# One channel chunk of an S4 inverse transform: products in fp32, fields summed on VectorE, a quarter of the matmuls

## The chip, the cores and the metric

The kernel runs on one core of a Trainium2 chip. The metric is the device time of one launch in microseconds (us). The core has five engines that run side by side, each in its own program order: TensorE (PE, matmuls; PEld is its weight load), VectorE (DVE), ScalarE (ACT), GpSimd (POOL) and SyncE (SP, which here issues nearly all DMAs). They wait for each other by semaphores.

## The reference

An S4 layer (a long convolution along the sequence, its kernel K built from complex exponentials) with a skip, then an MLP with layer norms, both added to the input. L = 2048, D = 512, N = 128 states, F = 1376.

```python
logdA = dt * A;  dB = dt * Bc
P = jnp.exp(logdA[:, :, None] * l[None, None, :])
K = jnp.einsum("dn,dnl,dn->dl", Cc, P, dB).real
...
Yf = Uf * Kf[None, :, :, :]
y = irfft2(Yf, ...)[:, :, 0, :L]
y = y.transpose(0, 2, 1) + u * Dskip[None, None, :]
...
x = A_u
h = x + _A_ref(_layernorm(x), ...)
h2 = h + _B_ref(_layernorm(h), B_w1, B_b1, B_w2, B_b2)
```

`_B_ref` normalizes once more, multiplies by w1 (512 to 1376), adds b1, takes a gelu, multiplies by w2 (1376 to 512) and adds b2.

## The kernel before

The sequence is cut into two blocks of 1024 rows (b = 0 and 1), the 512 channels into four chunks of 128 (`NCH = 4`, `CW = 128`). The convolution is done in a transformed domain by matmuls with small tables instead of an FFT. Up to about 105 us the kernel builds the convolution's kernel K (sines, exponentials, products: VectorE and ScalarE) and the forward transforms. Then, for each block and chunk, `inverse` multiplies transformed kernel and transformed input and transforms the product back. Block 0 needs one pair of fields (kernel, input). Block 1 needs two pairs, since its rows see both blocks of the input: (KF of block 0, input block 1) and (KF of block 1, input block 0).

`inverse(b, c, pairs, zt, pr)` works in two halves (`fh`) of 8 x 128 columns. A half is, for each pair and for `sw` 0 and 1, one multiply on VectorE of two bf16 fields of 128x1024 (L1193; with `sw` = 1 real and imaginary rows are swapped on one side) into a bf16 product tile. There are four product tiles `PR[0..3]`, used in turn, so a half of block 1 uses all four, and the next half's multiplies wait until TensorE has read them. Then come the matmuls that transform back (L1203): 16 per product tile, 64x128 each, 64 per half in block 1, all summed in one PSUM tile. The signs of the complex product are in the tables: rows r = 0 and 1 of a `sw` = 0 product go with the tables 0 and 1, both rows of a `sw` = 1 product with table 2. ScalarE (L517) or VectorE (L519) moves the PSUM tile to the tile Z, rearranged (128x128x8). After the second half, `turn` (L1219) lets SP issue a transposing DMA from Z to `ZT1[c]`.

When the four chunks of a block are done, `tail` (two per block, `sb`) makes the output of the convolution with the skip from the four ZT tiles (L1278), adds it to the input on VectorE (L1281), takes statistics (L1282, with a small power on POOL, L579), scales (L1293 or L1295) and transposes the result: by TensorE in the first tail of block 0 (L1305), by a `turn` elsewhere. `mlp` then has 11 column pieces of four matmuls each (L1321) with a gelu on ScalarE (L1323), and four row pieces of eleven matmuls each (L1337) with an addition on VectorE (L1339) and the DMAs to the output (L530). The MLP of block 0 is used as TensorE work between and behind the halves of block 1's inverse.

Every operation is recorded first, with a number in the order of recording. Then they are issued in an order written out as a table of numbers, `ORDER`: entry k stands for operation k // 2 on the first or second engine that it may take (k % 2), which settles whether a PSUM evacuation runs on ScalarE or on VectorE. An entry below zero is one "fill": a 128x512 matmul on the identity (L1434) that computes nothing. `SLOTS` gives the PSUM bank of each new PSUM tile. The cost numbers in `add` and its helpers serve the planner that wrote the table; no instruction depends on them.

The calls around the change, block 1's inverse and what follows it:

```python
    for c in range(NCH):
        inverse(1, c, [(KFb[0][c], XBc[c]), (KFb[1][c], XR[c])], ZT1[c], 17 + 0.1 * c)
    load_x(1, 16)
    mlp(0, 1, y2T[1], 18)
    tail(1, 0, y2T[2], 19)
```

Of the kernel before, what the change touches and what calls it, by code (L numbers as in the profile page):

```python
# [20 lines left out]
CW = 128  # L21
# [161 lines left out]
class VS(V):  # L183
# [28 lines left out]
    679, 578, 810, 808, 812, 542, 598, 1073, 510, 322, 624, 1079, -7, -7, -7, 702, 768, 520, 576, 512, 604, 528, 544, 536, 752, 554, 694, 308, 630,
    560, 814, 818, 826, 820, 390, 698, 754, 824, 696, 324, 706, 708, 710, 832, 688, 704, 690, 1082, 1084, 1086, 830, 326, 1080, 712, 868, 572, 700,
    1088, 1091, 822, 872, 750, 398, 564, 714, 716, 718, 720, 722, 874, 870, 834, 724, 1092, 1094, 1096, 888, 884, 1098, 1108, 726, 890, 904, 886, 756,
    880, 732, 1112, 736, 900, 828, 836, 876, 728, 882, 1111, 906, 920, 902, 878, 922, 744, 892, 848, 742, 839, 896, 850, 262, 738, 898, 392, 758,
    1100, 1102, 734, 1105, 730, 740, 932, 916, 788, 934, 918, 776, 912, 914, 1200, 936, 762, 786, 316, 894, 940, 780, 764, 924, 908, 910, 938, 1204,
    942, 944, 926, 856, 840, 1203, 858, 948, 950, 842, 972, 928, 956, 952, 782, 958, 860, 778, 930, 960, 964, 954, 946, 784, 864, 962, 974, 980, 966,
    770, 968, 970, 976, 774, 866, 863, 852, 1210, 982, 1212, 988, 854, 978, 844, 984, 760, 986, 990, 1214, 846, 996, 998, 1012, 772, 1114, 1140, 1142,
    1014, 1106, 1216, 1004, 1218, 1024, 1020, 1220, 1026, 1006, 1016, 1022, 1160, 1000, 992, 1116, 1002, 1124, 1126, 994, 1144, 1163, 1222, 1120,
    1164, 1146, 1122, 1008, 1152, 1225, 1010, 1018, 1028, 1030, 1038, 1032, 1034, 1166, 1156, 1158, 1154, 1206, 1256, 1258, 1260, 1036, 1040, 1048,  # L220
    1044, 1148, 1118, 1150, 1136, 1046, 1050, 1138, 1060, 1262, 1264, 1132, 1134, 1266, 1268, 1208, 1052, 1654, 1226, 1228, 1390, 1042, 1054, 1658,
    1312, 1062, 1271, 1272, 1656, 1231, 1274, 1232, 1392, 1276, 1236, 1394, 1279, 1234, 1652, 1239, 1240, 1242, 1056, 1282, 1284, 1128, 1176, 1178,
    1192, 1194, 1287, 1288, 1172, 318, 1131, 1320, 1322, 1175, 1314, 1188, 1190, 1280, 1168, 1170, 1660, 1662, 1324, 1665, 1327, 1244, 1246, 1316,
    1330, 1318, 1332, 1416, 1302, 1306, 1292, 1338, 1304, 1248, 1252, 1254, 1334, 1290, 1336, 1410, 1340, 1251, 1328, 1342, 1344, 1356, 1298, 1294,
    1296, 1348, 1180, 1196, 1358, 1360, 1182, 1350, 1301, 1376, 1374, 1198, 1362, 1352, 1628, 1366, 1396, 1354, 1368, 1648, 1378, 1650, 1370, 1644,
    1346, 1380, 1631, 1696, 1620, 1647, 1640, 1643, 1372, 1386, 1382, 1364, 1622, 1632, 1635, 1388, 1624, 1384, 1184, 1698, 1418, 1626, 1692, 1694,
    1420, 1666, 1430, 1186, 1426, 1402, 1428, 1422, 1432, 1668, 1670, 1310, 1798, 1308, 1796, 1678, 1636, 1424, 1434, 1436, 1438, 1404, 1440, 1638,
    1700, 1702, 1444, 1706, 1710, 1442, 1446, 1498, 1400, 1457, 1465, 1708, 1704, 1500, 1448, 1674, -2, -2, -2, -2, -2, -2, -2, -2, -2, -2, 1460,
    1712, 1467, 1468, 1802, 1473, 1476, 1676, 1458, 1462, 1452, 1480, 1474, 1398, 1724, 1479, 1718, 1720, 1672, 1470, 1454, 1486, 1722, 1714, 1492,
    1552, 1544, 1482, 1450, 1494, 1726, 1800, 1412, 1730, 1716, 1414, 1554, 1406, 1564, 1566, 1540, 1542, 1734, 1729, 1736, 1568, 1570, 1546, 1536,  # L230
    1538, 1556, 1732, 1680, 1684, 1738, 1683, 1488, 1686, 1558, 1548, 1532, 1688, 1560, 1744, 1746, 1484, 1408, 1550, 1748, 1750, 1740, 1496, 1528,
    1530, 1490, 1502, 1514, 1534, 1752, 1584, 1504, 1506, 1508, 1510, 1586, 1608, 1758, 1690, 1760, 1756, 1562, 1742, 1512, 1516, 1523, 1521, 1754,
    1518, 1762, 1588, 1524, 1764, 1770, 1776, 1772, 1596, 1774, 1610, 1766, 1598, 1600, 1778, 1782, 1572, 1526, 1780, 1590, 1808, 1784, 1844, 1768,
    1804, 1788, 1786, 1790, 1806, 1816, 1792, 1612, 1574, 1576, 1820, 1578, 1810, 1812, 1602, 1824, 1826, 1840, 1794, 1614, 1814, 1908, 1944, 1910,
    1912, 1896, 1822, 1914, 1902, 1962, 1818, 1898, 1904, 1916, 1950, 1842, 1900, 1956, 1592, 1906, 1918, 1920, 1922, 1836, 1952, 1838, 1832, 1828,
    1830, 1580, 1924, 1926, 1958, 1846, 1930, 1928, 1848, 1834, 1932, 1860, 1936, 1872, 1874, 1934, 1938, 1946, 1960, 1941, 1942, 1876, 1850, 1852,
# [1249 lines left out]
```

## Time and profile before

| | us |
|---|---|
| three runs | 243.19, 244.04, 246.56 |
| median | 244.04 |
| profiled execution | 245.59 |
| its span | 243.2 |
| TensorE busy | 215.4 (3696 matmuls) |
| VectorE busy | 179.6 (407 instructions) |
| ScalarE busy | 170.5 (232 instructions) |

The span is what the trace covers; the profiled execution's own time is 2.4 us longer. The page cuts the span into 40 slices of 6.08 us, and a digit is the busy share of an engine in a slice in tenths:

```profile
PE   7559786878988876979998999999999999999994
DVE  6999999999999995659998988797506991213022
ACT  3999999999999956975997987785134402903700
PEclk9999999999999999999999999999999999999999
```

The first 17 slices are the kernel's making and the forward transforms, with VectorE and ScalarE full. Block 0's inverse, tail and first MLP pieces and block 1's forward transforms follow, then from about 159 us (slice 27) on chunks 2 and 3 of block 1's inverse with MLP work, and from 186 us on block 1's tails and the rest of the MLP. "PEclk" is the granted TensorE clock in tenths of full speed.

### The profile page before, as it was taken

The numbers are of one execution on the slowest core, as the hardware profiler recorded it, in microseconds if no ns is written. First come the engines' busy times: TensorE is split into PE (matmuls) and PEld (weight loads), VectorE is DVE, ScalarE is ACT, GpSimd is POOL, SyncE is SP. The second block draws the span as 40 slices with busy tenths as digits, with TensorE's granted clock in tenths as the row PEclk, the third lists the DMA queues.
The fourth block names the chain that finished last, engine by engine and source line by source line (L and its number), as shares of the span: only waits on it lengthen the run. The fifth ranks groups of instructions, "written<-read, shape, count | busy, mean of one in ns | idle before, by whom it ended". The sixth has DMA issues, their size and how long they took to land.

```text
span 243.2 us, 8615 instructions
## 1 busy us (share of the span) xinstructions
PE 215.4 (89%) x3696; PEld 126.2 (52%) x3705; DVE 179.6 (74%) x407; ACT 170.5 (70%) x232; POOL 18.3 (8%) x145
## 2 busy tenths in 40 slices
PE   7559786878988876979998999999999999999994
PEld 2436243656634454755775476655554444444443
DVE  6999999999999995659998988797506991213022
ACT  3999999999999956975997987785134402903700
POOL 8800000011000000300000010010000101000000
PEclk9999999999999999999999999999999999999999
DMA  5121124000013943417899485644514051142303
GB/s 149 34 62 44 38 19 82 20 3 7 3 25 82 214 132 125 125 30 163 231 159 210 121 254 95 214 80 85 99 28 83 0 106 27 41 88 65 86 19 71
DMA packets 42448, 21.40 MB, mean 88 GB/s; under 512 B 30761, under 2 KB 40618, under 8 KB 42410
## 3 DMA queue, kind: packets, MB, share of 16 engines
q1 hardware_dynamic: 42250, 20.79, 38.0%
q8 instruction: 29, 0.48, 0.8%
q10 hardware_dynamic: 160, 0.07, 0.1%
q14 instruction: 9, 0.07, 0.1%
HBM read 10.33 MB, written 4.49 MB: 61 GB/s over the span
## 4 chain that ended last, share of the span: by engine, by line
PE 59%; DVE 26%; DMA 5%; issue 4%; SPq 3%; ACT 1%; DVEq 0%; ACTq 0%
PE ps L1321 16%; PE ps L1337 16%; PE ps L1203 7%; DVE ar L579 5%; DVE ar L519 4%; DMA ar<-ar 4%; PE ps L919 4%; PE ps L940 3%; DVE ar L1010 3%; SPq L530 3%; DVE ar L584 3%; PE ps L1054 3%; DVE ar L1031 3%; PE ps L1278 3%; PE ps L1055 2%
## 5 line engine op out<-in xcount | busy, mean ns | idle before, releaser
L517 ACT CAST ar<-ps 128x1024 bf16<-128x1024 f32 (+4 forms) x66 | 59.0, 941 | 16.7 <-PE ps L1203 7.5
L1323 ACT ACTIVATE ar<-ps,ar 128x512 bf16<-128x512 f32 (+1 forms) x44 | 27.6, 686 | 35.3 <-PE ps L1321 35.3
L1321 PE MATMUL ps<-ar 128*128 128x512 bf16 (+1 forms) x176 | 39.8, 379 | 0.0
L1337 PE MATMUL ps<-ar 128*128 128x512 bf16 (+2 forms) x179 | 38.5, 366 | 0.6 <-issue 0.3
L1339 DVE TENSOR_TENSOR ar<-ps,ar 128x512 bf16<-128x512 f32 (+1 forms) x17 | 10.8, 657 | 36.1 <-PE ps L1337 32.7
L519 DVE CAST ar<-ps 128x1024 bf16<-128x1024 f32 (+5 forms) x29 | 29.2, 1015 | 8.9 <-ACT ar L1029 2.8
L1193 DVE TENSOR_TENSOR ar<-ar 128x1024 bf16<-128x1024 bf16 x48 | 30.7, 685 | 6.5 <-PE ps L1203 6.0
L1337 PEld LDWEIGHTS <-ar 128*128 128x128 bf16 (+1 forms) x187 | 18.0, 98 | 19.6
L1321 PEld LDWEIGHTS <-ar 128*128 128x128 bf16 (+1 forms) x176 | 17.2, 100 | 20.4 <-issue 1.0
L1054 PE MATMUL ps<-ar 128*20 128x33 bf16 x512 | 20.0, 249 | 6.1 <-issue 5.6
L1203 PE MATMUL ps<-ar 64*128 64x128 bf16 x768 | 23.7, 216 | 0.1
L1203 PEld LDWEIGHTS <-ar 64*128 64x128 bf16 x768 | 21.5, 94 | 4.3 <-issue 2.1
L1029 ACT ACTIVATE ar<-ps 128x1024 bf16<-128x1024 int16 x20 | 19.6, 1039 | 3.0 <-issue 2.4
L579 POOL TENSOR_TENSOR ar<-ar 128x4 f32<-128x4 f32 (+1 forms) x6 | 7.4, 1226 | 187.5 <-DVE ar L584 149.3
L1010 DVE TENSOR_TENSOR ar<-ar 128x1024 bf16<-128x1024 bf16 x32 | 21.2, 684 | 0.2
L1055 PEld LDWEIGHTS <-ar 128*20 128x20 bf16 x512 | 17.7, 125 | 6.5 <-issue 6.4
L1055 PE MATMUL ps<-ar 128*20 128x33 bf16 x512 | 20.1, 248 | 0.0
L1054 PEld LDWEIGHTS <-ar 128*20 128x20 bf16 x512 | 17.6, 124 | 3.0 <-DVE ar L1031 1.5
L723 ACT ACTIVATE ar<-ar 128x512 bf16<-128x512 f32 x32 | 18.2, 628 | 0.5 <-DVE ar L565 0.5
L919 PE MATMUL ps<-ar 128*32 128x512 bf16 x256 | 15.7, 380 | 1.4 <-ACT ar L517 0.6
L1027 PE MATMUL ps<-ar 128*32 128x256 f16 (+2 forms) x288 | 13.5, 280 | 2.8 <-ACT ar L1029 2.7
L1031 DVE TENSOR_TENSOR ar<-ar 128x512 bf16<-128x512 bf16 x40 | 15.4, 413 | 0.3
(99 smaller groups left out, 284.6 us busy)
## 6 DMA issues: line engine op xcount, KB each, us to landing
ar<-in_A_u_dram SPq DMA_DIRECT2D x16, 128.0 KB
ar<-in_A_u_dram SPq DMA_DIRECT2D x8, 256.0 KB
out_dram<-ar SPq DMA_DIRECT2D x30, 64.0 KB
ar<-in_B_w_dram SPq DMA_DIRECT2D x4, 344.0 KB
ar<-in_B_w_dram SPq DMA_DIRECT2D x2, 640.0 KB
AK_d<-ar SPq DMA_DIRECT2D x2, 512.0 KB
ar<-AK_d SPq DMA_DIRECT2D x2, 512.0 KB
AKc_d<-ar SPq DMA_DIRECT2D x4, 256.0 KB
```

The lines of the kernel that those rows point to most:

```text
L517: act.copy(out_fn(), in_fn())
L519: dve.tensor_copy(out_fn(), in_fn())
L919: pe.matmul(pst(p)[32 * j:32 * j + 32, 512 * z:512 * z + 512], lhsT=BX.ap()[:, f0 + z, 16 - 16 * c:48 - 16 * c], rhs=src[2 * j + c].ap(), ...
L1010: add("DVE", c_dve(1024, 2), lambda e, lo=lo, rv=rv, sz=sc[z], e0=e0, o0=o0, q=q: dve.tensor_tensor(ent(o0, q, lo, 4, rv), ent(e0, q, lo, ...
L1031: add("DVE", c_dve(512, 2), lambda e, sc=sc, b0=b0, tb=tb, z=z: dve.tensor_tensor(tb[b0:b0 + 4].ap(), EA[c][b0:b0 + 4].ap(), sc[z].ap(), A ...
L1054: pe.matmul(o, lhsT=Ar.ap()[:, :, d], rhs=Br.ap()[:, :, d], start=True, stop=False, tile_position=(0, 32 * g))
L1055: pe.matmul(o, lhsT=Ai.ap()[:, :, d], rhs=Bi.ap()[:, :, d], start=False, stop=True, tile_position=(0, 32 * g))
L1193: dve.tensor_tensor(o, a, b_[:, :, ::-1, :] if sw else b_, ALU.mult)
L1203: pe.matmul(pst(p)[:, 512 * h + 128 * k:512 * h + 128 * k + 128], lhsT=q.ap()[rows, 2 * k + r, :], rhs=TP[w].ap()[rows, f0 // 2 + k, :], s ...
L1321: pe.matmul(pst(p)[:fs], lhsT=w1s[dc].ap()[:, fc * P:fc * P + fs], rhs=ybuf.ap().rearrange("p (t c) k -> p c t k", c=4)[:, dc], start=(dc ...
L1323: add("ACT", c_act(512, 1), lambda e, p=p, fc=fc, fs=fs: act.activation(hT.ap()[:fs, fc, :], pst(p)[:fs], ACT.Gelu_apprx_tanh, bias=b1_sb. ...
L1337: pe.matmul(pst(p)[:, c0:c1], lhsT=hT.ap()[:fs, fc, 128 * t:128 * t + 128], rhs=w2s[fc].ap()[:fs, c0:c1], start=(fc == 0), stop=(fc == NFC ...
```

## The change

For chunk 3 of block 1 alone, `inverse` takes another way through its products. Per half and per `sw`, both pairs are multiplied with an fp32 result (`mulf`), the two fp32 fields are added on VectorE, and a further VectorE operation on 512 elements takes the difference (`sw` = 0) or the sum (`sw` = 1) of its real and imaginary rows, rounded to bf16, into every second row of one product tile. That tile holds the finished complex product of both pairs, so one set of 16 matmuls with the tables 0 and 2 replaces the 64 of the half. Four bf16 multiplies per half on VectorE become four multiplies to fp32, two fp32 additions and two of 512 elements. The fp32 fields `XF` lie in place of `ZT1[3]`, which is written later, and of `PR[2]` and `PR[3]`; the product goes to `PR[1]` or `PR[0]`.

The other chunks of block 1 and all of block 0 compute as before. `on_dve=1`, a middle form, is used for no chunk.

```diff
     npr, nzw = [0], [0]
-
-    def inverse(b, c, pairs, zt, pr, on_pe=False):
+    XF = [at(ZT1[3].lo, f32, 8, CW), at(PR[2].lo, f32, 8, CW)]
+
+    def inverse(b, c, pairs, zt, pr, on_pe=False, on_dve=0):
...
-            for kf, X in pairs:
+
+            def mulf(kf, X, sw, o, f0=f0):
+
+                def f(e):
+                    a, b_, q = (v.ap().rearrange("p (a r) d -> p a r d", r=2) for v in (kf[f0:f0 + 8], X[f0:f0 + 8], o))
+                    dve.tensor_tensor(q, a, b_[:, :, ::-1, :] if sw else b_, ALU.mult)
+                add("DVE", c_dve(1024), f, r=[kf[f0:f0 + 8], X[f0:f0 + 8]], w=[o])
+                return o
+            if on_dve:
+                npr[0] += 1
+                o = PR[npr[0] % 2]
+                for sw in range(2):
+                    u, v = (mulf(kf, X, sw, XF[n]) for n, (kf, X) in enumerate(pairs))
...
+                        TT(u, u, v, ALU.add, pr=pr)
+                        part = lambda x, k: x.ap().rearrange("p (a r) d -> p a r d", r=2)[:, :, k, :]
+                        add("DVE", c_dve(512), lambda e, o=o, u=u, sw=sw: dve.tensor_tensor(part(o, sw), part(u, 0), part(u, 1), ALU.add if sw else ALU.subtract), r=[u], w=[o[k:k + 1] for k in range(sw, 8, 2)])
+                if on_dve == 2:
+                    jobs.append((o, 0, 2))
+            for kf, X in (() if on_dve else pairs):
...
-        inverse(1, c, [(KFb[0][c], XBc[c]), (KFb[1][c], XR[c])], ZT1[c], 17 + 0.1 * c)
+        inverse(1, c, [(KFb[0][c], XBc[c]), (KFb[1][c], XR[c])], ZT1[c], 17 + 0.1 * c, on_dve=2 if c in (3,) else 1 if c in () else 0)
```

The rest of the diff is the table. `ORDER` and `SLOTS` are written anew, and some cost numbers with them. A line or two of it, as an example:

```diff
-    94, 396, 382, 386, 78, 380, 0, 284, 72, 30, 32, 100, 2, 98, 38, 40, 96, 228, 4, 146, 42, 310, 138, 44, 76, 282, 102, 8, 200, 104, 300, 110, 118,
...
+    0, 30, 94, 396, 382, 2, 386, 78, 284, 32, 4, 8, 38, 6, 10, 380, 72, 100, 26, 282, 40, 300, 96, 98, 42, 82, 310, 44, 76, 12, 228, 102, 146, 80,
```

In it ScalarE's first 132 operations keep their order among themselves, VectorE's first 257, SP's first 89 and all of POOL's; TensorE's keep it up to there but for three pairs and for the fills, which are 35 for 28 in that part and 4 for 10 behind the first tail of block 0. From there on (about 105 us of the profile before) the order is another on TensorE, VectorE, ScalarE and SP. Lines of the changed kernel are some 25 higher: the multiplies of the other chunks stand at L1218, gelus at L1348, evacuations at L518 (ScalarE) and L520 (VectorE), the scale at L1318 or L1320.

VectorE, before: the multiplies of chunks 2 and 3 of block 1 (L1193), with statistics and scales of block 0's second tail (L584, L1293) and MLP additions (L1339) between.

```order
L1193 TENSOR_TENSOR ar<-ar 128x1024 x3
L584 TENSOR_SCALAR ar<-ar 128x4
L1293 TENSOR_SCALAR ar<-ar 128x512
L1193 TENSOR_TENSOR ar<-ar 128x1024
L1293 TENSOR_SCALAR ar<-ar 128x512
L1193 TENSOR_TENSOR ar<-ar 128x1024 x5
L1339 TENSOR_TENSOR ar<-ps,ar 128x512
L1193 TENSOR_TENSOR ar<-ar 128x1024 x3
L1339 TENSOR_TENSOR ar<-ps,ar 128x512 x3
```

The same place in the changed kernel: L1218 are chunk 2's multiplies, L1193 now the fp32 multiplies of chunk 3, L580 at 128x1024 the fp32 additions, L1208 the ones of 512 elements.

```order
L1218 TENSOR_TENSOR ar<-ar 128x1024 x4
L580 TENSOR_TENSOR ar<-ar 128x4
L585 TENSOR_SCALAR ar<-ar 128x4
L1318 TENSOR_SCALAR ar<-ar 128x512
L1193 TENSOR_TENSOR ar<-ar 128x1024
L1318 TENSOR_SCALAR ar<-ar 128x512
L1193 TENSOR_TENSOR ar<-ar 128x1024
L580 TENSOR_TENSOR ar<-ar 128x1024
L1208 TENSOR_TENSOR ar<-ar 128x4x128
L1193 TENSOR_TENSOR ar<-ar 128x1024 x2
L580 TENSOR_TENSOR ar<-ar 128x1024
L1208 TENSOR_TENSOR ar<-ar 128x4x128
```

The second half of chunk 3 repeats the last six kinds directly behind; the MLP additions that stood between the old multiplies come after it.

ScalarE, before, from the load of its gelu table (L511) on: L1323 are gelus, L517 at 128x1024 evacuations of forward transforms or kernel fields, at 128x128x8 those of an inverse half.

```order
L511 ACT_TABLE_LOAD
L1323 ACTIVATE ar<-ps,ar 128x512 x3
L1323 ACTIVATE ar<-ps,ar 96x512
L1323 ACTIVATE ar<-ps,ar 128x512 x2
L517 COPY ar<-ps 128x1024
L1323 ACTIVATE ar<-ps,ar 128x512
L517 COPY ar<-ps 128x1024
L1323 ACTIVATE ar<-ps,ar 128x512
L517 COPY ar<-ps 128x128x8
```

ScalarE, in the changed kernel, from the same load on: L518 are evacuations, L1320 scales, L1348 the gelus.

```order
L512 ACT_TABLE_LOAD
L518 COPY ar<-ps 128x128x8
L1320 ACTIVATE ar<-ps,ar 128x512
L518 COPY ar<-ps 128x512
L1320 ACTIVATE ar<-ps,ar 128x512 x2
L518 COPY ar<-ps 128x512
L518 COPY ar<-ps 128x128x8
L518 COPY ar<-ps 128x512 x4
L518 COPY ar<-ps 128x128x8
L518 COPY ar<-ps 128x1024 x2
L1348 ACTIVATE ar<-ps,ar 128x512
L518 COPY ar<-ps 128x1024 x2
```

The evacuations of three inverse halves and the first tail's scales stand between the table load and the first gelu, where three gelus followed the load directly. VectorE's evacuations 1024 wide ahead of chunk 3's products fall from 12 to 9.

29 lines of the change are left out of this document (17 added, 12 removed), and 85 rows, old and new, of the table ORDER.

## The prediction

> **What bounds the kernel now.** I read the busy time by stretches first, then the chain of waits, then VectorE's row of the timeline. The first view gives busy time per engine (count of instructions in brackets), the granted TensorE clock, the DMA share and GB/s.
>
> ```profile
> core 0: us, PE busy (x) PEld busy (x) DVE busy (x) ACT busy (x) POOL busy (x), PEclk, DMA share, GB/s
> 0.00:105.00 105.00, 83.62 (x1984) 52.03 (x1988) 97.09 (x260) 95.14 (x131) 14.30 (x141) 1.00 0.29 69
> 105.00:141.00 36.00, 33.60 (x821) 22.03 (x820) 30.86 (x48) 29.04 (x34) 0.14 (x1) 1.00 0.74 161
> 141.00:163.50 22.50, 22.50 (x369) 13.95 (x368) 19.49 (x36) 18.24 (x26) 1.09 (x2) 1.00 0.59 150
> 163.50:186.00 22.50, 22.08 (x266) 12.54 (x272) 10.61 (x19) 8.43 (x12) 0.78 (x1) 1.00 0.45 86
> 186.00:240.00 54.00, 53.63 (x272) 25.62 (x275) 21.27 (x47) 19.66 (x32) 2.01 (x2) 1.00 0.26 53
> ```
>
> Up to 105 us VectorE and ScalarE are full (97.09 and 95.14 of 105) and TensorE is not. From 141 us on TensorE is never idle to speak of: 98.2 of 99 us. So a microsecond of TensorE work that goes after 141 us is a microsecond of the end, as long as what feeds TensorE keeps up. Between 163.5 and 186 VectorE has 10.61 of 22.5 us busy, so 11.9 us are free. The chain of waits (start, length, what) names the pieces:
>
> ```profile
> 139.13 1.89 PE ps L1203 x64
> 141.02 0.34 PE ps L1278 x2
> 141.36 2.26 PE ps L1434 x10
> ...
> 161.59 1.89 PE ps L1203 x64
> ...
> 166.83 1.89 PE ps L1203 x64
> ...
> 172.07 1.89 PE ps L1203 x64
> 173.96 0.16 issue
> 174.12 0.81 PE ps L1337 x3
> 174.93 2.59 PE ps L1321 x12
> 177.52 1.89 PE ps L1203 x64
> 179.42 0.97 PE ps L1321 x4
> ...
> 186.01 3.58 PE ps L1278 x32
> ```
>
> L1203 are the halves of the second block's inverse transforms: chunk 2 ends with the one at 166.83, chunk 3 is at 172.07 and 177.52. L1321 and L1337 are MLP matmuls that lie between, 0.216 us each (12 in 2.59). L1434 are ten filling matmuls that compute nothing, 2.26 us. And VectorE in the same stretch:
>
> ```profile
> 163.31 1.91 DVE L1193 TENSOR_TENSOR ar<-ar 128x1024 bf16<-128x1024 bf16 x3
> 165.14 0.15 DVE L584 SCALAR_TENSOR_TENSOR ar<-ar 128x4 f32<-128x4 f32 x1
> 165.33 0.41 DVE L1293 TENSOR_SCALAR ar<-ar 128x512 bf16<-128x512 bf16 x1
> 165.66 0.68 DVE L1193 TENSOR_TENSOR ar<-ar 128x1024 bf16<-128x1024 bf16 x1
> 166.26 0.40 DVE L1293 TENSOR_SCALAR ar<-ar 128x512 bf16<-128x512 bf16 x1
> 168.43 2.50 DVE L1193 TENSOR_TENSOR ar<-ar 128x1024 bf16<-128x1024 bf16 x4 [1.77 <-PE ps L1203]
> 173.67 0.69 DVE L1193 TENSOR_TENSOR ar<-ar 128x1024 bf16<-128x1024 bf16 x1 [2.74 <-PE ps L1203]
> ```
>
> Four multiplies take 2.50 us, then VectorE waits until TensorE has read the four product tiles: the two engines take turns, and MLP work fills TensorE's side of it.
>
> **TensorE's gain.** Each half of chunk 3 falls from 64 matmuls to 16. At 1.89 us for 64 that is 0.47, so 2 x 1.42 = 2.84 us go. Of the ten fills after the first block's tail four stay; six at 0.226 are 1.36 us, which go only if nothing then waits there. The first 105 us get seven more fills (35 for 28), 1.5 us, at places where TensorE waits for ScalarE and VectorE, whose own order is unchanged there. I cost that at nothing; without the cover it is 1.5 us. The planner's new cost numbers reach no instruction.
>
> **VectorE's price.** Eight multiplies at 2.50/4 leave. Per half come four multiplies that read bf16 and write fp32, two fp32 sums of 1024, and two that take 2x512 fp32 to 512 bf16. No row has the first form; the nearest are these (mean ns of one after the busy time; the last row is two in a row on the timeline):
>
> ```profile
> L519 DVE CAST ar<-ps 128x1024 bf16<-128x1024 f32 x17 | 20.6, 1219 | 6.0 <-ACT ar L1029 2.8 <-PE ps L1169 1.8 <-PE ps L940 1.4
> L579 DVE TENSOR_TENSOR ar<-ar 128x256 f32<-128x256 f32 x16 | 6.4, 415 | 0.0
> L579 DVE TENSOR_TENSOR ar<-ps,ar 128x256 f32<-128x256 bf16 x10 | 3.8, 403 | 0.2 <-ACT ar L591 0.2
> L1031 DVE TENSOR_TENSOR ar<-ar 128x512 bf16<-128x512 bf16 x40 | 15.4, 413 | 0.3
> 131.51 2.36 DVE L519 CAST ar<-ps 128x1024 bf16<-128x1024 f32 x2 [0.93 <-PE ps L940]
> ```
>
> An fp32 operation on 256 takes what a bf16 one takes on 512, so fp32 runs at half the bf16 rate. Bf16 operands with an fp32 result (403 ns for 256, one from PSUM) go with the slow ones. At the slow rate 1024 elements take 2.36 - 1.22 = 1.14 us from start to start. So a multiply costs between 0.61 (the bf16 pace, (2.50 - 0.69)/3) and 1.14; I take 1.14. The section "What auto-detection actually checks" of the Trainium skill's page "VectorE: DVE Perf Modes" says the fast two-operand mode needs every tensor in 16 bits, result included; by that the eight multiplies are slow, and by a rule that asked for 16-bit operands alone they would be 4.2 us cheaper. The trace has only the 403 ns row for it, which agrees.
>
> The 16 instructions then take 12 x 1.14 + 4 x 0.60 = 16.1 us. Eight of them use the result of the one just before and have to wait for its end, 1.22 - 1.14 = 0.08 later, some 0.1 with the hand-over: 0.9. Together 17.0 us for 5.0. Only the first may start before chunk 2's second half is read, since the second writes over that half's product tile: 15.9 us follow that half. One scale of the first block's tail (0.40) stands inside.
>
> **What VectorE sheds and when it gets there.** Ahead of the block its 1024-wide PSUM evacuations fall from 12 to 9 (3 x 1.14 = 3.4 us, to ScalarE), 512-wide ones rise by two (2 x 0.60), and one scale gets cheaper: 2.5 us less. The stretch before:
>
> ```profile
> 104.20:166.70 62.50, 60.05 (x1219) 37.78 (x1210) 54.28 (x92) 50.34 (x64) 2.01 (x2) 1.00 0.65 150
> DVE ar L519 <- PE ps L1055: 2.2, 1, 2.2
> DVE ar L519 <- PE ps L1169: 1.8, 2, 1.5
> DVE ar L1193 <- PE ps L1203: 1.5, 3, 0.9
> DVE ar L519 <- PE ps L940: 1.4, 2, 0.9
> ```
>
> VectorE was busy 54.28 and idle 8.2 us. The last 0.9 us (tail arithmetic and scale) follow chunk 2's last multiply, so after the change that multiply ends at 104.2 + 54.3 - 2.5 - 0.9 = 155.1 plus its waits. With all 8.2 us: 163.3. TensorE gives the other end: it now reaches chunk 2's second half with 31 MLP matmuls (6.7 us) and the six fills moved from ahead of it, 166.83 - 6.7 - 1.36 = 158.8. I take 6 us of waits, 161.1: the waits on L1055 and L940 (3.6) stem from work that is not touched, those on L1169 go with the evacuations, and taking turns costs more, since the MLP work that lay between the halves is now behind them, some 0.4 us at each of five turns.
>
> **The sum.** Chunk 2's second half 161.1 + 1.9 = 163.0; the block ends at 178.9; chunk 3's second half starts at 179.0. Without a wait TensorE would be there at 177.52 - 1.42 - 1.36 + 8 x 0.216 (two MLP pieces net ahead of it) = 176.5, so it loses 2.5 us. From 177.52 to TensorE's end at
>
> ```profile
> 230.57 9.29 PE ps L1337 x53
> 239.88 0.42 DVE ar L1339
> ```
>
> 239.88 are 62.4 us; less 1.42 and the 1.73 moved ahead, 59.2. TensorE ends at 238.2 instead of 239.9: 1.7 us sooner. Behind chunk 3 come evacuation and the transposing DMA of its result, then the tail's matmuls (L1278 at 186.01): 30 MLP matmuls, 6.5 us, cover it as 6.6 us did, so it costs nothing. The next such DMA, for the tail's own output, has 13.8 us of TensorE work where it had 14.8, and VectorE is spared two 0.69 us additions ahead of it; nothing, or 1 us if that fails. The SP queue sends the first block's weight and input loads in another order; all are asked for over 10 us ahead of use, so nothing again. The profiled execution took 245.59 us (span 243.2, 2.4 around it), 1.55 over the median of 244.04; 1.7 off is 243.9 for it, and 242.4 against the median.
>
> **Rivals.** *TensorE stays full.* VectorE gets through with 3.7 us of waits or less, or the multiplies run at 0.61. Chunk 3's second half starts at 176.5, TensorE ends at 235.7, 4.2 us sooner: 239.9. The stretch before 141 holds the wait for a transposing DMA, which issues earlier now; up to 2 us more, 237.9. For it: 11.9 idle us in the stretch where 12.0 are added. Against: they were idle because the halves were spread out.
>
> *VectorE is late.* One mechanism, the four product tiles of the inverse: each half's multiplies wait for the reading of the half before, and TensorE now waits for them in turn. From 162.9 us on as the start of chunk 2's second half the gain is gone (162.9 + 17.8 = 180.7 = 239.9 - 59.2). With before's 8.2 us of waits and 2 to 3.5 more, 165.3 to 166.8, chunk 3 starts at 183 to 184.7: slower by 2.4 to 4 us, 246.5 to 248. For it: three of five covers shrink. Against: VectorE has less to do.
>
> *The clock falls.* With six fills gone TensorE idles some 1.4 to 2.3 us before the first MLP. The granted clock is 1.00 in every stretch now, and only the first matmuls are slow:
>
> ```profile
> L1449 PE MATMUL ps<-ar 1*128 1x512 bf16 x8 | 3.8, 622 | 1.4 <-POOL ar L1442 1.4
> ```
>
> At that pace 3.4 us of work, an inverse half and MLP, take twice as long: 245.8. The page "TensorE: Matmul & The Clock Gate" of the Trainium skill, Part 1, halves the clock only after an idle window of about 3.4 us. Nothing in this trace idles so long.
>
> **Chances.** Forecast 0.54 (240.9 to 244.0), TensorE full 0.25, VectorE late 0.17, clock 0.04. The range 238.3 to 246 takes in the forecast, most of the first rival and the milder part of the others. A measurement of this kernel tells about 2% from no change, here under 239.2 and over 248.9: faster 0.16 (the better part of the first rival), slower 0.08 (VectorE late at its worst, with the fp32 operations dearer than taken), within 2% 0.76.
>
> **What would show it.** The fp32 multiplies at about 1.2 us a record; VectorE all but gapless from the first MLP to chunk 3's last sum, at 178 to 180; a TensorE wait for VectorE ahead of the two short halves or the chunk 2 halves, 2 to 4 us in all; no idle ahead of L1278's second block. A last sum before 176 or after 181 would make the number wrong, and so would a first stretch that is not the same within 0.5 us.

## The result and the profile after

The changed kernel takes 242.38 us (median of 20 runs, 241.13 to 243.94), the kernel before 244.25 us (20 runs, 241.94 to 246.56). The ratio is 0.9946, with a 95% interval from 0.9922 to 0.9970: 0.7 to 1.9 us faster by the ratio, 1.9 by the medians. Medians here and below count every execution, while a ratio leaves out those more than 1.5% above the fastest of their kernel. The profiled execution took 242.12 us, with a span of 240.3.

The busy time by the same stretches as before, with the same columns:

```profile
0.00:105.00 105.00, 87.19 (x2010) 53.74 (x2013) 98.25 (x261) 95.77 (x132) 14.30 (x141) 1.00 0.30 69
...
141.00:163.50 22.50, 21.09 (x414) 13.99 (x412) 21.17 (x40) 18.81 (x27) 1.39 (x1) 1.00 0.47 99
163.50:186.00 22.50, 22.25 (x135) 10.37 (x137) 16.88 (x20) 10.14 (x16) 0.00 (x0) 1.00 0.57 109
```

In the last of these stretches VectorE went from 10.61 to 16.88 us busy and TensorE stayed full (22.25 of 22.5). What is new is in the one before it: TensorE lost 1.4 us where it had lost none. The chain of waits, with the halves of the inverse now on L1228 and block 1's tail on L1303:

```profile
145.75 1.96 PE ps L1228 x64
...
150.45 1.89 PE ps L1228 x64
...
154.86 1.89 PE ps L1228 x64
...
159.45 1.89 PE ps L1228 x64
...
173.53 0.55 PE ps L1228 x16
...
177.42 0.56 PE ps L1228 x14
...
184.57 3.58 PE ps L1303 x32
...
236.79 0.42 DVE ar L1364
```

Chunk 2's second half starts at 159.4 where it started at 166.8. Chunk 3's halves take 0.55 us in place of 1.89 (the second has its first two matmuls at 177.16). VectorE's groups by form, the first row chunks 0 to 2 and all of block 0, the other three the new block:

```profile
L1218 DVE TENSOR_TENSOR ar<-ar 128x1024 bf16<-128x1024 bf16 x40 | 25.5, 686 | 1.3 <-PE ps L1228 1.0
L1193 DVE TENSOR_TENSOR ar<-ar 128x1024 f32<-128x1024 bf16 x8 | 9.5, 1219 | 0.0
L580 DVE TENSOR_TENSOR ar<-ar 128x1024 f32<-128x1024 f32 x4 | 4.9, 1225 | 0.1
L1208 DVE TENSOR_TENSOR ar<-ar 128x512 bf16<-128x512 f32 x4 | 2.8, 692 | 0.1
```

And the ends of the block on VectorE's timeline:

```profile
156.63 2.49 DVE L1218 TENSOR_TENSOR ar<-ar 128x1024 bf16<-128x1024 bf16 x4
...
159.83 1.22 DVE L1193 TENSOR_TENSOR ar<-ar 128x1024 f32<-128x1024 bf16 x1
...
176.67 0.69 DVE L1208 TENSOR_TENSOR ar<-ar 128x512 bf16<-128x512 f32 x1
178.84 2.48 DVE L1364 TENSOR_TENSOR ar<-ps,ar 128x512 bf16<-128x512 f32 x4 [1.47 <-PE ps L1362]
```

Chunk 2's last multiply ends at 159.1, the block runs from 159.8 to 177.4 with gaps of 0.2 us in all. TensorE came to chunk 3's second half at 177.16: a dead heat.

**The same stages in both.** Two single executions can't be laid side by side from their starts, because the stretch up to about 105 us varies from run to run (last section). A mark right behind it serves better: the first of the 96 matmuls on L1109 (L1110 after), at 107.67 and 106.44. Cut from there at chunk 0's two halves, chunk 1's first, chunk 2's second, chunk 3's second and TensorE's end, first the kernel before:

```profile
107.67:139.06 31.39, 30.01 (x679) 18.83 (x678) 28.61 (x40) 26.15 (x30) 0.00 (x0) 1.00 0.79 167
139.06:143.78 4.72, 4.72 (x83) 3.10 (x82) 4.49 (x13) 3.49 (x5) 1.01 (x1) 1.00 0.89 267
143.78:149.05 5.27, 5.27 (x93) 3.46 (x92) 4.88 (x9) 5.02 (x9) 0.00 (x0) 1.00 0.32 92
149.05:166.76 17.71, 17.66 (x275) 10.53 (x275) 14.95 (x29) 13.06 (x19) 1.01 (x1) 1.00 0.57 135
166.76:177.46 10.70, 10.38 (x160) 6.55 (x161) 5.59 (x9) 3.00 (x4) 0.00 (x0) 1.00 0.53 100
177.46:239.84 62.38, 62.12 (x365) 30.30 (x369) 23.04 (x49) 22.77 (x36) 2.01 (x2) 1.00 0.28 57
sum 132.17, PE 130.15 PEld 72.76 DVE 81.57 ACT 73.49 POOL 4.03; mean PE 21.69 PEld 12.13 DVE 13.59 ACT 12.25 POOL 0.67
```

and the changed kernel:

```profile
106.44:136.94 30.50, 29.15 (x669) 18.68 (x669) 27.88 (x40) 26.16 (x30) 0.00 (x0) 1.00 0.86 183
136.94:141.39 4.45, 3.47 (x74) 2.31 (x73) 4.20 (x13) 3.41 (x4) 1.55 (x1) 1.00 0.95 233
141.39:145.75 4.36, 3.12 (x81) 2.75 (x80) 4.36 (x8) 4.36 (x8) 0.00 (x0) 1.00 0.32 96
145.75:159.38 13.63, 13.46 (x256) 8.41 (x257) 12.41 (x26) 10.50 (x15) 1.39 (x1) 1.00 0.66 127
159.38:177.16 17.78, 17.57 (x150) 8.93 (x152) 17.46 (x19) 9.63 (x14) 0.00 (x0) 1.00 0.49 90
177.16:236.69 59.53, 59.28 (x310) 28.36 (x313) 23.63 (x51) 21.25 (x33) 2.01 (x2) 1.00 0.29 59
sum 130.25, PE 126.05 PEld 69.43 DVE 89.95 ACT 75.32 POOL 4.96; mean PE 21.01 PEld 11.57 DVE 14.99 ACT 12.55 POOL 0.83
```

From the mark to the end: 132.17 and 130.25, so 1.92 us less. Not all of it is gain: eight matmuls of 128x256 (L940, L941 after) that stand behind the mark in the kernel before stand ahead of it in the changed one, and they took 0.56 us there. For equal work the trace shows about 1.4 us, close to the 1.3 in the middle of the ratio's interval. TensorE is busy 4.10 us less, these 0.56 included, and idle 2.18 us more (4.20 for 2.02). The new idle time lies in the second and third stage, 0.98 and 1.24 us. From chunk 1's first half on TensorE has 0.6 us of idle time in 91.

### The profile page after: what moved, and what is told of

It is laid out like the page before. It is cut to its first block, busy times and chain, and to the rows that moved or that the text cites. A ratio compares the mean times of both kernels' runs of the same rounds, so it can differ in the third digit from the quotient of the medians.

```text
span 240.3 us, 8440 instructions
## 1 busy us (share of the span) xinstructions
PE 214.7 (89%) x3603; PEld 124.4 (52%) x3610; DVE 188.7 (79%) x414; ACT 172.5 (72%) x233; POOL 19.3 (8%) x145
## 4 chain that ended last, share of the span: by engine, by line
PE 50%; DVE 14%; ACT 14%; DMA 11%; SPq 6%; issue 3%; DVEq 0%
PE ps L1362 16%; PE ps L1346 16%; SPq L531 5%; PE ps L1228 5%; DVE ar L580 4%; PE ps L941 4%; ACT ar L724 3%; ACT ar L1001 3%; DVE ar L585 2%; ACT ar L518 2%; PE ps L1055 2%; PE ps L1056 2%; DMA ar<-AL_d 2%; DMA ar<-AKc_d 2%; PE ps L920 2%
## 5 line engine op out<-in xcount | busy, mean ns | idle before, releaser
L518 ACT CAST ar<-ps 128x1024 bf16<-128x1024 f32 (+4 forms) x69 | 62.5, 947 | 11.4 <-PE ps L1228 3.4
L1348 ACT ACTIVATE ar<-ps,ar 128x512 bf16<-128x512 f32 (+1 forms) x44 | 28.0, 687 | 34.2 <-PE ps L1346 27.5
L1362 PE MATMUL ps<-ar 128*128 128x512 bf16 (+3 forms) x181 | 39.1, 366 | 0.4 <-issue 0.2
L520 DVE CAST ar<-ps 128x1024 bf16<-128x1024 f32 (+5 forms) x26 | 25.2, 975 | 4.6 <-PE ps L1056 2.5
L1346 PEld LDWEIGHTS <-ar 128*128 128x128 bf16 (+1 forms) x176 | 17.2, 100 | 20.6 <-issue 1.3
L1218 DVE TENSOR_TENSOR ar<-ar 128x1024 bf16<-128x1024 bf16 x40 | 25.5, 686 | 1.3 <-PE ps L1228 1.0
L580 POOL TENSOR_TENSOR ar<-ar 128x4 f32<-128x4 f32 (+1 forms) x6 | 8.3, 1382 | 180.2 <-DVE ar L585 147.6
L1056 PE MATMUL ps<-ar 128*20 128x33 bf16 x512 | 20.5, 248 | 2.5 <-issue 2.5
L1228 PE MATMUL ps<-ar 64*128 64x128 bf16 x672 | 21.2, 217 | 1.0 <-DVE ar L1218 1.0
L1011 DVE TENSOR_TENSOR ar<-ar 128x1024 bf16<-128x1024 bf16 x32 | 21.4, 687 | 0.6 <-ACT ar L1001 0.5
L1228 PEld LDWEIGHTS <-ar 64*128 64x128 bf16 x672 | 18.8, 94 | 5.8 <-DVE ar L1218 2.4
L1030 ACT ACTIVATE ar<-ps 128x1024 bf16<-128x1024 int16 x20 | 19.6, 1046 | 2.3 <-issue 1.6
L1055 PE MATMUL ps<-ar 128*20 128x33 bf16 x512 | 20.4, 249 | 0.3 <-ACT ar L968 0.3
L580 DVE TENSOR_TENSOR ar<-ar 128x256 f32<-128x256 f32 (+13 forms) x43 | 18.4, 442 | 0.5
L1001 ACT ACTIVATE ar<-ps 128x1024 bf16<-128x1024 int16 x16 | 15.2, 1045 | 1.0 <-PE ps L993 1.0
```

Source lines behind the costliest of these rows:

```text
L518: act.copy(out_fn(), in_fn())
L520: dve.tensor_copy(out_fn(), in_fn())
L580: add(eng, tuple(c[q] for q in eng), lambda e: (dve if e == "DVE" else gp).tensor_tensor(oap() if oap else o.ap(), aap() if aap else a.ap( ...
L1001: add("ACT", c_act(1024), lambda e, p=p, sc=sc, cs=cs: act.activation(sc[cs].ap().rearrange("p a b -> p (a b)"), pst(p, i16).rearrange("p ...
L1055: pe.matmul(o, lhsT=Ar.ap()[:, :, d], rhs=Br.ap()[:, :, d], start=True, stop=False, tile_position=(0, 32 * g))
L1056: pe.matmul(o, lhsT=Ai.ap()[:, :, d], rhs=Bi.ap()[:, :, d], start=False, stop=True, tile_position=(0, 32 * g))
```

## The experiments

Each run stands beside runs of the kernel before on the same chip. "Changed" is the changed kernel. The stages are those above, in us, each read from the starts of the matmuls in that run's trace. Stage 1, from the mark to chunk 0's first half, is not in the table.

| run | median us | ratio to before (95%) | 2: chunk 0, 1st to 2nd half | 3: to chunk 1, 1st | 4: to chunk 2, 2nd | 5: to chunk 3, 2nd | 6: to the end | mark to end |
|---|---|---|---|---|---|---|---|---|
| before | 244.25 | | 4.72 | 5.27 | 17.72 | 10.69 | 62.39 | 132.2 |
| changed | 242.38 | 0.9946 (0.9922 to 0.9970) | 4.45 | 4.36 | 13.63 | 17.78 | 59.53 | 130.3 |
| order_only | 245.41 | 1.0023 (0.9984 to 1.0062) | 4.45 | 4.36 | 13.63 | 19.12 | 60.66 | 132.8 |
| change_only | 252.34 | 1.0214 (1.0142 to 1.0285) | 4.72 | 5.27 | 17.71 | 15.39 | 64.49 | 138.6 |
| fields_bf16 | 241.85 | 0.9885 (0.9845 to 0.9925) | 4.45 | 4.36 | 13.63 | 17.78 | 59.32 | 130.2 |
| block_longer | 246.39 | 1.0077 (1.0036 to 1.0117) | 4.45 | 4.36 | 13.63 | 17.78 | 62.04 | 133.2 |
| tail_light | 242.89 | 0.9981 (0.9941 to 1.0021) | 4.45 | 4.33 | 13.63 | 17.78 | 59.52 | 129.9 |
| six_tiles | 242.21 | 0.9939 (0.9900 to 0.9978) | 4.45 | 4.13 | 13.63 | 17.78 | 59.52 | 129.7 |
| six_light | 241.60 | 0.9901 (0.9853 to 0.9950) | 4.45 | 3.70 | 13.63 | 17.78 | 59.53 | 129.6 |
| fills10 | 243.59 | 0.9999 (0.9961 to 1.0038) | 5.75 | 4.33 | 13.63 | 17.78 | 59.53 | 131.7 |
| pe16_before | 241.49 | 0.9885 (0.9838 to 0.9933) | 4.72 | 5.27 | 17.72 | 9.35 | 61.39 | 132.3 |
| two_chunks | 243.58 | 0.9999 (0.9965 to 1.0033) | 4.45 | 4.36 | 21.28 | 11.86 | 58.67 | 131.7 |
| two_chunks_six | 242.84 | 0.9942 (0.9906 to 0.9978) | 3.50 | 5.09 | 21.28 | 11.95 | 58.67 | 130.7 |
| two_chunks_v2 | 249.24 | 1.0217 (1.0163 to 1.0270) | 3.50 | 5.07 | 30.84 | 10.18 | 58.67 | 138.4 |

Wherever the order is the same and no edit acts on them, stages 2 to 6 repeat to within 0.3 us, most to 0.01. So a stage of one run shows what the interval of a run's time leaves open. Stage 1 does not repeat so well: it takes 30.1 to 31.0 us in the traces of the new order, 31.4 and 31.0 in `before` and `change_only`, and 33.9 in `pe16_before`, where TensorE's granted clock was 0.50 from 108 to 114 us. The last column holds this, so single traces tell it to about 1 us, and for `pe16_before` it says nothing on the edit.

### The order and the products, apart

`order_only` is the changed table with chunk 3 as it was. In the table (entry = twice the operation's number):

```diff
-    ... 1770, ... 1772, 1406, 1774, 1776,
-    1780, 1778, 1782, 1784, 1792, 1544, 1790, 1794, 1796, 1800, 1596, 1798, 1802, 1523, 1804, ...
+    ... 1770, 1772, 1406, 1776, 1774,
...
+    ... 1778, 1782, 1784, 1786, 1788,
```

> The changed kernel's order and PSUM banks with chunk 3 as it was: four bf16 multiplies and 64 matmuls per half, the fp32 operations left out; the second half's multiplies stand behind the first half's matmuls. TensorE gets 2 x 1.42 = 2.84 us of matmuls back, VectorE loses its block of 17.5 us. Forecast's reading (the block kept TensorE waiting for 2.5 us): +2.84 - 2.5 = 0.3 us over the changed kernel, 242.7. Rival (the block ended just as TensorE came to the half, 0.2 us of waiting at most, and what TensorE saved was lost in other places): +2.84 - 0.2 = 2.6 over the changed kernel, 245.0, so slower than before by about 0.8. A third reading, in which the saved matmuls were never on the path, gives 242.4.

245.41 us, 0.6 over before by the ratio (0.4 under to 1.5 over), which the 245.0 of the second reading fits. Stage 5 took 1.34 us more than in the changed kernel and stage 6 1.13 more. So of the 2.68 us that the 96 matmuls cost (two halves at 1.34), removing the VectorE block won back 0.2. The expectation had put the forecast's loss of 2.5 us wholly on that block; the prediction's own times put 2.3 of it ahead of chunk 2's second half (161.1 for 158.8) and 0.2 at the block. Only the latter is what this run tests, and it bears it out.

`change_only` is the changed code in the table of before, two new operations in the place of each old multiply:

```diff
-    ... 1770, 1776, 1772, 1596, 1774, 1610, ...
+    ... 1770, 1772, 1774, 1776, 1778, 1780, 1596, 1782, 1784, 1610, ...
```

> The changed products of chunk 3 in the order before, each old multiply replaced in its place by two of the new operations. Both theories: VectorE gets to the block only after chunk 2's second half is read (168.7 in the profile before), the block takes 15.9 us from there and one MLP addition of 0.7 stands inside, so it ends near 185.3; TensorE came to the second half at 177.52 and saves 1.42 in each half, so the end moves by 185.3 - 177.5 - 1.4 = 6.4 us: about 250.6. Rival: VectorE's 11.9 us of idle time in that stretch cover the block wherever it stands, and TensorE's saving comes through: 244.25 - 2.84 = 241.4.

252.34 us by the median; the ratio gives 5.2 more (3.5 to 7.0), and from the mark to the end it is 6.4 more. Rival refuted: free time on VectorE is no cover where TensorE has its own work elsewhere in its queue. TensorE's wait list between 160 and 190 us:

```profile
PE ps L1228 <- DVE ar L1208: 7.4, 2, 4.1
```

Two waits, 7.4 us, one in each short half behind its first two matmuls. So neither part alone gains (the order makes no clear difference, the products cost 5 to 6 us) and both together gain 1.3 to 1.9: the new order has carried 31 MLP matmuls behind chunk 2, where they cover the block.

### The block and its cover

`fields_bf16` makes the block about half as long:

```diff
-    XF = [at(ZT1[3].lo, f32, 8, CW), at(PR[2].lo, f32, 8, CW)]
+    XF = [at(ZT1[3].lo, bf16, 8, CW), at(PR[2].lo, bf16, 8, CW)]
```

> The changed kernel with bf16 in place of fp32 for the fields between the multiplies and the product, same order. At 0.61 us a multiply or sum of 1024 and some 0.35 for 512, with 0.9 for the hand-over, the block takes about 9.6 us in place of the 17.5 of the profile. Forecast's reading (TensorE loses 2.5 us to the block): 2.5 less, 239.9. Rival (TensorE comes to the second half just as the block ends): 0.2 less, 242.2. A block of fp32 that is not slow at all would leave both times and the block's length as they are, but the profile's 1219 ns a multiply already speak against it.

VectorE's groups in this run:

```profile
L1193 DVE TENSOR_TENSOR ar<-ar 128x1024 bf16<-128x1024 bf16 x8 | 5.2, 684 | 0.4 <-PE ps L1228 0.4
L580 DVE TENSOR_TENSOR ar<-ar 128x1024 bf16<-128x1024 bf16 x4 | 2.8, 692 | 0.1
L1208 DVE TENSOR_TENSOR ar<-ar 128x512 bf16<-128x512 bf16 x4 | 1.7, 424 | 0.1
```

17.2 us of work became 9.7, stage 5 stayed at 17.78 and stage 6 fell from 59.53 to 59.32: the fp32 block costs 0.2 us where it stands. The multiply went from 1219 to 684 ns with nothing but the type of its result changed. That is what the Trainium skill's page "VectorE: DVE Perf Modes" (What auto-detection actually checks) says, and what the forecast took at 1.14 from start to start.

`block_longer` does two of the multiplies twice, in the loop of the multiply:

```diff
+                    for _ in range(2 if f0 == 0 and sw else 1):
-                    dve.tensor_tensor(q, a, b_[:, :, ::-1, :] if sw else b_, ALU.mult)
+                        dve.tensor_tensor(q, a, b_[:, :, ::-1, :] if sw else b_, ALU.mult)
```

> The changed kernel with the two sw = 1 multiplies of chunk 3's first half done twice, 2 x 1.14 = 2.3 us more on VectorE in the block, nothing else. If the block's end is what chunk 3's second half starts on (177.36 in the profile, TensorE there at 177.2), all but 0.2 us of it shows at the end: 2.1 to 2.3 more, 244.5 to 244.7. If there is cover that the profile doesn't show, less; with 2 us or more of cover, 242.4.

TensorE's timeline around chunk 3's second half:

```profile
179.70 0.23 PE L1229 MATMUL ps<-ar 64*128 64x128 bf16 x2
182.47 0.57 PE L1229 MATMUL ps<-ar 64*128 64x128 bf16 x14 [2.54 <-DVE ar L1209]
```

TensorE did the two matmuls that the first part of the product feeds, then sat idle for 2.54 us for the 2.4 added, and stage 6, which holds this wait, grew by 2.51. So the dead heat is real: there is no slack at the block's end, and only 0.2 us is lost to it. By the ratios the time is 3.2 over the changed kernel (1.31%, with intervals of 0.4% and 0.2% either way); the trace shows 2.5 of it as the block's.

### TensorE's terms

`pe16_before`:

```diff
+                use = jobs[:1] if b == 1 and c == 3 else jobs
                 for k in range(4):
-                    for n, (q, w0, w1) in enumerate(jobs):
+                    for n, (q, w0, w1) in enumerate(use):
...
```

> The kernel before with only the first 16 of the 64 matmuls in each half of chunk 3 (the other three product tiles of that chunk are left out); its four multiplies per half stay, order and banks are those of before. TensorE loses 2 x 1.42 = 2.84 us and VectorE gains no work. If TensorE sets the end from 141 us on (98.2 of 99 us busy): 2.84 less than before, 241.5. If chunk 3's halves wait for their multiplies instead (the second half's products come 2.5 us after the first half is read, with 3.4 us of MLP matmuls between): the same 241.5. If the saved time is lost to the transposing DMAs or the gelus behind: 244.3.

241.49 us, 2.8 less by the ratio (1.6 to 4.0). Stages 5 and 6 show 1.34 and 1.00; the slow clock in stage 1 of this trace hides it in the last column. In the profiles a half saves 1.34 (1.89 to 0.55) rather than the 1.42 of the forecast.

`fills10`:

```diff
-    ... -3, -3, -3, -3, ...
+    ... -3, -3, -3, -3, -3, -3, -3, -3, -3, -3, ...
```

> The changed kernel with ten fills in place of four behind block 0's first tail, as the kernel before had. The forecast counted the six fills at 0.226 as 1.36 us of TensorE's time ahead of chunk 2. The profile of the changed kernel shows the four fills from 140.44 to 141.35 and chunk 0's second half at 141.39, its multiplies done at 141.17, so only 0.2 us of cover: by this 1.1 to 1.4 more, 243.5 to 243.8. If the turns behind them have slack, 242.4.

Stage 2 took 5.75 for 4.45, 1.30 of the 1.36, and the ratio puts the run 1.3 over the changed kernel. The six fills were worth what they cost. But in the changed kernel stage 2 is only 0.27 shorter than before, since TensorE waits there now.

### Where TensorE's 2.2 us go

TensorE's wait list of the changed kernel from 140 to 190 us:

```profile
PE ps L1459 <- ACT ar L518: 1.0, 1, 1.0
PE ps L1228 <- DVE ar L1218: 1.0, 1, 1.0
```

The fills (L1459) wait for ScalarE's evacuation, then chunk 1's first half for its products; 0.3 us more of stage 3 is another wait for ScalarE (L1330). Theory A blamed turn-taking over the four product tiles all the way from chunk 0 to chunk 2, theory B the amount of VectorE's work. `tail_light`, with m = 256 in block 0's second tail and 512 elsewhere:

```diff
-... dve.tensor_tensor(hh.ap(), pst(p), hh.ap(), ALU.add) ...
+... dve.tensor_tensor(hh.ap()[:, :m], pst(p)[:, :m], hh.ap()[:, :m], ALU.add) ...
-... dve.bn_stats(st2[8 * b + j].ap(), pst(p) if first else hh.ap()) ...
+... dve.bn_stats(st2[8 * b + j].ap(), (pst(p) if first else hh.ap())[:, :m]) ...
```

> The changed kernel with the four additions and four statistics of block 0's second tail on 256 of 512 columns (half of that tail's sum and statistics is left out), which takes 8 x 0.27 = 2.2 us off VectorE between 142 and 157 us, while it is busy all but 0.9 us of that stretch. Theory A (turn-taking: from chunk 0's first half at 136.9 to chunk 2's second at 159.4 lie five turns of 2.5 us multiplies and 1.96 us matmuls, 22.3 of the 22.4 us, and the tail's work lies inside the matmuls' time): 0 to 0.3 less than the changed kernel, 242.1 to 242.4. Theory B (VectorE's amount of work sets when chunk 2's second half starts): TensorE has 1.9 us to win there, so 1.9 less, 240.5.

`six_tiles`:

```diff
+    PRX = PR + [at(ZT1[3].lo + 2048 * n, bf16, 8, CW) for n in range(2)]
...
-                    pr_ = PR[npr[0] % 4]
+                    pr_ = PRX[(npr[0] - 12) % 6] if b else PR[npr[0] % 4]
```

> The changed kernel with six product tiles in place of four for chunks 0 to 2 of block 1 (the two more lie where the fp32 field lies later), same order. Two multiplies of a half no longer wait until the half before is read. Theory A (turn-taking): the turns shorten until VectorE is full, and it is idle for 0.9 us there: 0.5 to 0.9 less, 241.5 to 241.9. Theory B (VectorE's amount of work): 0 less, 242.4, at most 0.3.

`six_light` is both edits:

> Both together: six product tiles and the lighter tail (half of that tail's sum and statistics left out). Theory A: now neither the tiles nor VectorE's work hold the turns, and TensorE can win up to the 1.9 us that it loses there: 1.5 to 1.9 less than the changed kernel, 240.5 to 240.9, and more than the two single gains together. Theory B: as the lighter tail alone.

Stage 4 of the lighter tail, then stages 3 and 4 of both edits:

```profile
145.41:159.04 13.63, 13.46 (x256) 8.41 (x256) 11.03 (x27) 10.54 (x15) 1.01 (x1) 1.00 0.67 127
```

```profile
141.24:144.94 3.70, 3.12 (x81) 2.80 (x81) 3.70 (x8) 3.70 (x7) 0.00 (x0) 1.00 0.51 158
144.94:158.58 13.64, 13.47 (x258) 8.42 (x258) 11.38 (x28) 10.94 (x15) 1.39 (x1) 1.00 0.72 128
```

Both theories fell on stage 4. It takes 13.63 us whether VectorE has 12.41 or 11.03 us of work and with four tiles or six: TensorE is busy 13.46 of it and sets it alone. In stage 3 A is right on a small scale: the lighter tail alone wins 0.03, six tiles alone 0.23, both 0.66 of the 1.24 us of idle time, not 1.5 to 1.9. So there the tiles and the tail's work on VectorE (L1318, L1306) held the products back for nearly the same time. Why the fills wait for ScalarE in stage 2 wasn't settled; without fills (below) stage 2 fell to 3.50 and stage 3 rose to 5.09, so that wait mostly moved.

### The same for chunk 2

If TensorE is full and bf16 fields leave 7.5 us free on VectorE, a second chunk could follow. Its order was written by hand: 20 MLP matmuls stand ahead of chunk 2's first half in place of 8, and 31 between its halves in place of 12. By operations of the table that is three and five more (the expectation's 15 is a miscount).

```diff
-on_dve=2 if c in (3,) else 1 if c in () else 0
+on_dve=2 if c in (2, 3) else 1 if c in () else 0
...
-    XF = [at(ZT1[3].lo, f32, 8, CW), at(PR[2].lo, f32, 8, CW)]
+    XF = [at(ZT1[3].lo, bf16, 8, CW), at(PR[2].lo, bf16, 8, CW)]
```

> The change carried on to chunk 2 as well: chunks 2 and 3 of block 1 by the new way, fields in bf16 (VectorE some 9.6 us a chunk), with 15 MLP matmul groups moved ahead of chunk 2's halves by hand. The marks say that TensorE is full from chunk 1's first half (145.75) to the end in the changed kernel, so another 2 x 1.42 = 2.84 us of matmuls come off the end if VectorE keeps up: 239.6, to 240.1 with 0.5 of waits. Rival: chunk 2's products take 4.8 us in place of 2.5 in each half and the MLP work ahead does not cover it: up to 4.6 lost, 2.84 won, 244.2.

243.58 us. VectorE kept up; two other waits of TensorE took the place of the gain:

```profile
PE ps L1362 <- ACT ar L1348: 1.7, 1, 1.7
PE ps L1346 <- DMA ar<-ar: 1.5, 1, 1.5
```

a gelu, which stood behind a scale on ScalarE, and the transposing DMA of block 0's second tail, whose scales had been put behind the new products. `two_chunks_six` has the edit of `six_tiles` (with + 2 for - 12) and no fills:

> The kernel with two chunks, with six product tiles for chunks 0 and 1 and without the four fills behind block 0's first tail. In the run with six tiles the stretch from chunk 0's second to chunk 1's first half fell from 4.36 to 4.13 us; without fills the one ahead of it (4.45) can fall by up to 0.5. So 0.2 to 0.7 less than two chunks alone, 239.0 to 239.4; the same if the wait for ScalarE ahead of the fills is only renamed.

242.84 us, ratio as the changed kernel's. `two_chunks_v2` puts the scales sooner and chunk 1's transposing DMA ahead of that tail's:

> The kernel with two chunks, six product tiles and no fills, its order mended where its trace showed new waits: all four scales of block 0's second tail on VectorE and some 5 us sooner, so that the transposing DMA to the second MLP no longer lands after TensorE comes to it (1.5 us), chunk 1's own DMA ahead of it, and gelus ahead of evacuations where TensorE waited for one (1.7 us). If TensorE is then full from chunk 1's first half on: 90.9 us of the changed kernel from there to the end, less 2.84, and 0.2 from the six tiles, so 3.0 less than the changed kernel: 239.4 (239.2 to 239.9). Rival: a wait of the same kind comes up at another bank, gelu or DMA, as in the first two tries: 241 to 242.5.

249.24 us, a miss of 10. SP's timeline:

```profile
143.99 17.37 SPq L1245 DMA_TRANSPOSE ar<-ar  x3
...
163.12 0.59 SPq L531 DMA_DIRECT2D ar<-in_B_w_dram  x1
```

In `two_chunks_six` and in the changed kernel that weight load was issued at 148.0 and 149.0, ahead of these transposes. Behind them it came at 163.1, and TensorE's wait list shows the price:

```profile
PE ps L1363 <- DMA ar<-in_B_w_dram: 7.4, 1, 7.4
```

The transposes held the queue because they stood there waiting for their data: issuing one takes 1.5 to 2.0 us in this trace, but between the end of the first and the start of the second lie 9.7. Behind the gap of 7.4 us TensorE's granted clock was about 0.5 until 174.7 us: stage 4 is 9.6 us longer than in `two_chunks_six`, 6.8 of it idle time and 2.8 longer busy time. Whether the second chunk gains with that load in front stays open; it wasn't tried. No kernel here is clearly faster than the changed one: `fields_bf16` has a lower ratio, but its interval overlaps and its stages are equal but for 0.2 us. `six_light` leaves work out.

## Why the prediction was right, and where not

**The total.** Forecast 1.7 us less, measured 1.9 by the medians, 1.3 by the ratio of the runs, and about 1.4 for equal work behind the mark. The profiled execution went from 245.59 to 242.12, further than the 243.9 forecast for it, mainly because the mark came 1.23 sooner; traces of the new and the old order have the mark at 105.7 to 108.6 and at 104.3 to 107.7, so nothing shows that part to be the change's. For the same reason these traces can't tell whether the seven more fills at the front cost something: that they are free is neither refuted nor shown.

**TensorE's gain** was forecast at 2.84 + 1.36 = 4.2. The experiments show its terms one by one: 2.34 to 2.48 for the two halves (stages 5 and 6 of `pe16_before` and `order_only`), with 1.34 a half for 1.42, and 1.30 for the six fills (`fills10`), so 3.6 to 3.8. The busy time fell by 4.10, but that holds the eight matmuls that went ahead of the mark.

**VectorE's price** was right: 1219 ns a record for about 1.2, and the block took 17.5 us from its first multiply (159.83 to 177.36) for 17.0 plus the scale inside, which the forecast names but leaves out of its 178.9. The share behind chunk 2's second half, with the start of that half, gave 17.9 to chunk 3's second half; 17.78 measured.

**The failed step** is "I take 6 us of waits, 161.1", which let VectorE set the start of chunk 2's second half 2.3 us behind TensorE's own pace. The size was nearly right: counted from the same distance to the mark (102.97 us for the forecast's 104.20), VectorE was busy 50.8 us up to chunk 2's last multiply and idle 5.4, where the forecast had 50.9 and 6. The path was not: TensorE waits for no product in stage 4, which is its own alone (13.46 of 13.63 busy, the same with 1.4 us less on VectorE). What stood in its place: 0.98 and 1.24 us ahead of chunk 1's first half, a wait for ScalarE in front of the fills, which no step had, and one turn over the product tiles with the tail's work beside it, where the forecast had five turns. That the sum came out is in part luck: a loss of 2.2 stood where 2.3 had been taken, at another place and for another reason.

**The rivals.** TensorE is full from chunk 1's first half on, as the first rival had it; its price left out the idle time ahead of that half. "VectorE is late" didn't come about, but `change_only` and `block_longer` show its mechanism at chunk 3: every microsecond by which the block ends later is a microsecond of the end. The clock didn't fall behind the four fills. It did in the experiments, after longer idle time: in `change_only`, the stretch behind a gap of 4.15 us (168.52 to 172.67), then a gap of 3.26 us and the stretch behind it:

```profile
172.67:175.00 2.33, 2.33 (x20) 1.15 (x21) 2.33 (x3) 1.01 (x1) 0.00 (x0) 0.72 0.00 0
178.64:181.90 3.26, 0.00 (x2) 0.01 (x2) 3.13 (x4) 0.62 (x1) 0.00 (x0) 1.00 0.00 0
181.90:184.00 2.10, 2.10 (x22) 1.17 (x23) 0.00 (x0) 1.50 (x2) 0.00 (x0) 1.00 0.00 0
```

The granted clock fell behind the first gap and stayed behind the second. The Trainium skill's page "TensorE: Matmul & The Clock Gate" (Part 1) puts the window at about 3.4 us, which lies between the two; the last section has falls behind shorter gaps, which that figure does not cover.

**What should have shown it.** The block's end at 178 to 180 was at 177.4, or 178.6 with the mark laid on that of before. One sign that the forecast named against its number did appear: the first stretch was not the same within 0.5 us (the mark came 1.23 us sooner). The forecast for the profiled execution missed by 1.8 us, the one for the median held. The waits of 2 to 4 us for VectorE ahead of chunk 2 or the short halves were not there (1.0 ahead of chunk 1). TensorE ran into block 1's tail without a wait (184.57), as said.

## What to carry to other kernels

Work moved from a full engine to a free one is paid for where the free engine's result is awaited: the same products gained with 31 matmuls of other work in front and cost 5 to 6 us without. Behind a mark at which runs meet, most stages of this statically ordered kernel repeat to hundredths of a microsecond, so one trace can settle what many timed runs can't; first make sure that the same work stands behind the mark in both, and that the granted clock is the same. A DMA that waits in its queue for its data holds up everything queued behind it; count that when an order is rewritten.

## What was not expected of the hardware

Most of the spread between the traces arises between 85 us and the mark: ScalarE's 115th instruction starts at 84.7 to 85.9 us in all fourteen, the mark lies at 104.3 to 108.6. In this stretch ScalarE and TensorE pause where no other engine and no buffer releases them. The kernel before had the longest such pause on ScalarE:

```profile
89.24 1.03 ACT L1029 ACTIVATE ar<-ps 128x1024 bf16<-128x1024 int16 x1 [2.41 <-issue]
```

In `change_only`, the same order, that instruction waited 0.84 us, and the mark came 3.3 us sooner. The pauses have fixed places in the program. ScalarE's falls on this one instruction in eight traces. TensorE has 47 pauses of 0.3 us or more with no releaser in the fourteen traces, up to 1.95 us, and all stand a multiple of 128 matmuls apart (to within two records, and some are missing in a trace). With a weight load for each matmul that is a period of 256 instructions. In the same stretch the queue that loads the program moves packets of 16 KB, four of them between 84 and 104 us in the kernel before (packets, MB, share of the DMA engines):

```profile
q8 instruction: 4, 0.07, 1.3%
```

This points to the loading of the program as the cause of the pauses; no run here tests it.

In four runs TensorE's clock was then halved, for some 3 us in `order_only`, `block_longer` and `six_tiles` and for 7 in `pe16_before`, though the longest gap between its matmuls there was 1.23, 1.94, 1.95 and 0.89 us. The first of them:

```profile
96.00:97.00 1.00, 1.00 (x19) 0.83 (x20) 0.54 (x2) 0.00 (x0) 0.00 (x0) 0.75 0.11 37
97.00:98.00 1.00, 1.00 (x10) 0.48 (x8) 0.96 (x3) 0.65 (x1) 0.00 (x0) 0.50 0.18 53
```

Full speed was back at 100 us. The clock was also halved from 15 to 20 us in `order_only`, `six_light` and `two_chunks_v2`, behind a gap of 2.83 us at 12 us; the other runs, with 2.32 us or less there, kept full speed. What makes the difference to the gap of 3.26 us after which the clock stayed was not tried.
